# Top-32 attention and a low-rank mixer on one core: the order of the last attention step, and who turns three results of the seventh batch

## Chip, core, metric

The kernel runs on one core of one Trainium2 chip. The metric is the device time of one execution in microseconds, median of several runs. All data are float32.

## What is computed

Attention with batch B = 8, H = 8 heads, S = 576 rows, head width D = 64, where every query keeps its 32 largest scores, followed by a mixer with a low-rank product over the rows and a two-layer MLP over the 512 channels.

```python
scores = (1.0 / np.sqrt(D)) * np.matmul(q, k.transpose(0, 1, 3, 2))
kth = np.partition(scores, -32, axis=-1)[..., -32:-31]
scores = np.where(scores >= kth, scores, -1e9)
attn = np.exp(scores - np.max(scores, axis=-1, keepdims=True))
attn = attn / (np.sum(attn, axis=-1, keepdims=True) + 1e-09)
x = np.matmul(attn, v)                    # then (B, H, S, D) -> (B, S, H*D)
h = x.transpose(0, 2, 1) @ U @ V          # U: 576 x 32, V: 32 x 576
u = x + h.transpose(0, 2, 1)
return u + np.maximum(u @ w_ch1, 0.0) @ w_ch2     # 512 x 2048, 2048 x 512
```

## The kernel before

**Tiles and steps.** The 64 heads are handled as 32 pairs g of two heads (four pairs to a batch). A pair's 576 query rows are cut into four tiles of 128 rows, t = 0 to 3, and a tail of 64 rows, t = 4. From the second batch on, one step n of the main loop (line 1221) starts one tile; a pair's fourth tile and its tail share a step. STEPS is the number of steps; the loop runs two steps more, n = STEPS and STEPS + 1, in which nothing new begins and the last tiles are finished. Below, "(31,2)" is tile 2 of the last pair.

**One tile.** TensorE forms the scores (L350, the tail's L382), ScalarE copies them (L395, L415, L418), VectorE finds the 32 largest by rounds of MAX8 and MATCH_REPLACE8 (L500 to L539), ScalarE and GpSimd push everything below the smallest of them far down (L571, L572), and ScalarE takes the exps with their sums (L453), the tail's last, and adds a tiny number to the sums `den` of all nine columns of the pair (L582). The exps must be turned for the product with v. For the four tiles of a late pair, `blocks` does it: VectorE transposes 32x32 blocks into `y` (L598, three instructions, one buffer), SyncE writes `y` to DRAM in four DMAs (`away<-y`, L604), and `back` reads it into `PT` through ScalarE's queue (L613). The tail is turned by TensorE (L634, L639) and copied by ScalarE (L635, L640); the generator `turned` does that piece by piece, at each `turn()`. `values` multiplies with v (L708, L711; the tail's L682) and ScalarE copies the result to `XT` (L720, L689).

**The sums.** `inverse` takes the reciprocal of the pair's sums (L651), turns them (L653) and writes them to DRAM in four DMAs on SyncE's queue (L657). `scale` reads them back, spread over 64 partitions each, in two DMAs on ScalarE's queue (L668).

**The mixer.** `mixed(g, wait, lag)` is a generator. GpSimd multiplies XT by the scale (L740 twice, L743 twice, into `uT`), TensorE turns uT (L750, the tail's L761), ScalarE copies it to X (L754, L762), then `wait` calls of `fill()` go by; then TensorE's product with U (L773), ScalarE's copy (L781), TensorE's two products with V (L785), ScalarE's copies (L800) and GpSimd's sums into uT (L801). For the last pair it is called as `mixed(g, 5, 0)`, and when it ends it starts the closing.

**The MLP as filling.** The MLP of a batch whose four pairs are done runs as a generator `mlp(b)` while later pairs are worked on. `fill()` moves `mixing[0]` on by one piece and then draws products from the first generator in `fillers` until a share is used up, at the end of the kernel 1.02 x 512 columns, two products of 256 columns. So the place and number of the `fill()` calls decide how many products (L845 first layer, L862 second layer) stand between two pieces of attention work on TensorE, whose order is exactly the order of emission. In the second half of `mlp(6)`, the seventh batch (256 of its 576 rows), four results of 128 channels come out, c = 0 to 3, of 16 products each. For each, ScalarE copies the sum (L873), GpSimd adds uT (L874), and 12 products later `turned_back` runs: TensorE turns it in two transposes (L886), ScalarE copies it to `ob` (L888), and SyncE stores it in one DMA (L892).

**The closing.** The eighth batch's MLP (`closing`, started by the end of the last pair's mixer) uses a scheme with seven block products instead of eight; it begins with sums by VectorE (L963 to L966) and by GpSimd (L931 to L934, into `raw`), and its products are all on L938, two instructions of 288 columns to each. A round of its first half is products x, y, z, x, y, z and, a round later, a fourth z; between them VectorE (L1057, L1063, L1066, L1034) and GpSimd (L1067) combine parts. Its results are turned by VectorE in 32x32 blocks (`give`, L1123) and stored in pieces of 32 rows (L1128, L1132), the last three by TensorE (L1140).

**Order and waits.** Every engine runs its instructions in the order in which the Python code emits them. A DMA is issued by the queue of the engine that it is written on and stands in that engine's order. All DMAs of SyncE and ScalarE together are given one of eight semaphores in turn; a DMA waits until the DMA before it on its semaphore has landed.

The end of the loop body for n >= STEPS, in the order of the code: `next(last)` moves the last tiles' exps on, `here` is empty. Step STEPS works on the exps of (31,3) and the tail, the blocks of (31,3), the products of (31,1) at its start and of (31,2) in `weighted(n - 2)`. Step STEPS + 1 turns the tail, reads the blocks of (31,3) back and multiplies.

Of the kernel before, what the change touches and what calls it, by code (L numbers as in the profile page):

```python
# [8 lines left out]
F32 = mybir.dt.float32  # L9
# [17 lines left out]
def kernel(  # L27
# [28 lines left out]
    nc = tc.nc  # L56
    B, H, S, D = q.shape
    P = 128
# [4 lines left out]
    NT, TAIL = 4, 64  # L63
    MAIN = NT * P
    HALF = S // 2
    assert S == MAIN + TAIL and D == 64 and H % 2 == 0 and C == 512 and TOPK % 8 == 0
    NPAIR = H // 2
    NP = B * NPAIR

    CH = NT + 1  # L70
    ALONE = NPAIR * CH
# [4 lines left out]
    BLK = 32  # L76
# [8 lines left out]
    mlpp = ctx.enter_context(tc.tile_pool(name="mlpp", bufs=2))  # L85
# [524 lines left out]
    def back(g, t):  # L610

        if (g, t) in aways:
            nc.scalar.dma_start(  # L613
                PTs[g, t].rearrange("p a n -> p (a n)"),
                aways.pop((g, t)).rearrange("p a n -> p (a n)"),
            )
# [44 lines left out]
    def scale(g):  # L661

        rd = scales.pop(g)
        sc = attn.tile([P, TAIL + S], F32, tag="scale", name="scale", bufs=1)
        scales[g] = sc
        flat = rd.rearrange("r n -> () (r n)")
        for h in range(2):
            nc.scalar.dma_start(  # L668
                sc[half(h), (1 - h) * TAIL : (1 - h) * TAIL + S],
                flat[:, h * S : (h + 1) * S].to_broadcast([D, S]),  # L670
            )
# [156 lines left out]
    def mlp(b):  # L828

        uT = uTs[b]  # L830
        for chunks, (lo, hi) in zip(PARTS, SPAN):
# [27 lines left out]
            for c in range(NC):  # L859
# [15 lines left out]
                later(12, turned_back(b, chunks, lo, c, oT))  # L875
                yield w / C

    def turned_back(b, chunks, lo, c, oT):


        def run():
            cs = slice(c * P, (c + 1) * P)
            tp = ps_t.tile([P, 3, P], F32, tag="tp", name="tp")
            for i, t in enumerate(chunks):
                n = rows(t)
                nc.tensor.transpose(tp[0:n, i, :], oT[:, OFF[t] - lo : OFF[t] - lo + n], ident)  # L886
            ob = mlpp.tile([P, 3, P], F32, tag="ob", name="ob", bufs=2)
            nc.scalar.copy(ob[:, 0:2], tp[:, 0:2, :])  # L888
            if NT in chunks:
                nc.scalar.copy(ob[0:TAIL, 2], tp[0:TAIL, 2, :])  # L890
            t = chunks[0]
            nc.sync.dma_start(  # L892
                out[b, 0:MAIN, cs].rearrange("(p t) c -> p t c", t=NT)[:, t : t + 2, :],
                ob[:, 0:2],
            )
            if NT in chunks:
                nc.sync.dma_start(out[b, MAIN:S, cs], ob[0:TAIL, 2])

        return run
# [267 lines left out]
    def fill(k=1):  # L1167


        nonlocal due  # L1170
        for _ in range(k):
            if passes:
                passes.pop(0)()
            if mixing and next(mixing[0], True):
                mixing.pop(0)
            part = share * (LONG if len(tiles(n)) > 1 else 1)
            if n <= ALONE + BATCH + 2:
                part *= EARLY[min(max(n - ALONE, 0) // NT, NT - 1)]
            due += part
            while due > 0:  # L1180
                if not fillers:
                    due = 0.0
                    break
                done = next(fillers[0], None)
                if done is None:
                    fillers.pop(0)
                elif not done:
                    due = 0.0
                else:
                    due -= done  # L1190

    def tiles(n):

        return steps[n] if 0 <= n < STEPS else []

    def weighted(m):

        for g, t in tiles(m):
            values(g, t)
        if tiles(m)[-1][1] == NT:  # L1200
            mixing.append(mixed(g, None, 1 if g > NPAIR + 1 else 4) if m < STEPS - 1 else mixed(g, 5, 0))

    def turn():

# [16 lines left out]
    for n in range(STEPS + 2):  # L1221
        if n < STEPS:
            g, t = steps[n][0]
            if t == 0 and g < NPAIR:
                load(g + 1)
            if t == (1 if g < NPAIR else 2) and g + 1 < NP:
                ready = prep(g + 1)
            fronts[n] = front(steps[n])
            next(fronts[n])
            if owed:  # L1230
                inverse(owed.pop(), 0, 2 * NT + 1)
        else:
            t = NT
        here, last = fronts.get(n, iter(())), fronts.pop(n - 1, iter(()))
        if n >= ALONE - 1 and n <= ALONE:

            if n < ALONE:
                next(last)
                values(*steps[n - 3][0])
                list(turning)  # L1240
                next(here)
                next(last)
                scores(*steps[n + 1][0])
                fold(*steps[n + 1][0])
                values(*steps[n - 2][0])
            list(turns(*steps[n - 1][0]))
            values(*steps[n - 1][0])
            if n < ALONE:
                split(*steps[n + 1][0])
                next(here)  # L1250
                next(here)
                inverse(g, 0, 2 * NT)
                mixing.append(mixed(g, 1))
                fill()
                next(here)
                continue
            fill()
            scores(*steps[n + 1][0])
            fold(*steps[n + 1][0])
            next(here)  # L1260
            while mixing:
                fill()
            next_params(1)
            fill()
            next(last, None)
            next(here)
            fill()
            split(*steps[n + 1][0])
            next(here)
            coming = loading(g + 1)  # L1270
            next(coming)
            next(coming)
            next(here)
            fill()
            continue
        if n < ALONE:
            ease = n > 0 and eased(*steps[n - 1][0])
            if ease:
                next(last, None)
            scores(*steps[n + 1][0])  # L1280
            fold(*steps[n + 1][0])
            if n >= 3:
                values(*steps[n - 3][0])
                if (n - 3) % CH == NT:
                    mixing.append(mixed((n - 3) // CH, 3))
            list(turning)
            fill()
            next(here)
            if t < NT - 1:
                next_params(1)  # L1290
            fill()
            next(ready, None)
            next(here)
            next(last, None)
            fill()
            split(*steps[n + 1][0])
            next(here)
            if t < NT:
                next_params(1)
            next(here)  # L1300
            fill()
            if n >= 1:
                turning = turns(*steps[n - 1][0])
            continue
        next(last, None)
        fill()
        if ALONE <= n - 3 <= STEPS - 3:
            weighted(n - 3)
            if waiting:
                waiting.clear()  # L1310
                if next(mixing[0], True):
                    mixing.pop(0)
        for tile_ in tiles(n + 1):
            if tile_[1] < NT:
                scores(*tile_, len(tiles(n + 1)) > 1)
            fold(*tile_)
        turn()
        fill()
        turn()
        next(last, None)  # L1320
        for tile_ in tiles(n - 2):
            back(*tile_)
        fill()
        turn()
        fill()
        next(last, None)
        if n < STEPS and n - 2 >= ALONE and len(tiles(n - 2)) > 1:
            scale(steps[n - 2][0][0])
        next(here, None)
        if g == NPAIR:  # L1330
            next_params(1)
        fill()
        if n >= STEPS:
            if n == STEPS:
                inverse(NP - 1, 0, 2 * NT + 1)
                scale(NP - 1)
            weighted(n - 2)
        next(here, None)
        for tile_ in tiles(n + 1):
            split(*tile_)  # L1340
        fill()
        next(here, None)
        for tile_ in tiles(n - 1):
            if shared(*tile_):
                blocks(*tile_)
        turning = turned(n - 1)
        if n < STEPS and n - 1 >= ALONE and len(tiles(n - 1)) > 1:
            owed.append(steps[n - 1][0][0])
            if owed[0] > NPAIR + 1:
                inverse(owed.pop(), 0, 2 * NT + 1)  # L1350
        if n < STEPS:
            if t == NT - 1:
                coming = loading(g + 2) if g + 2 < NP else iter(())
            next(coming, None)
        next(ready, None)
        if t < NT - 1:
            next_params(1)
        next(here, None)
        fill()
        fill()  # L1360
# [35 lines left out]
```

## Time and profile before

| | us |
|---|---|
| median of 4 runs | 1650.68 |
| the 4 runs | 1650.25, 1650.84, 1650.52, 1653.97 |
| the profiled execution | 1650.25 |
| its span, first to last instruction | 1648.5 |
| TensorE busy in it | 1555.8 (94%) |
| VectorE busy | 1543.3 (94%) |
| GpSimd busy | 1009.3 (61%) |
| ScalarE busy | 994.3 (60%) |

The stretches of the end, in us from the span's start; the granted clock of TensorE is 1.00 in all of them but the last (0.89).

| stretch | long | TensorE busy | VectorE | ScalarE | GpSimd | what it holds |
|---|---|---|---|---|---|---|
| 1480 to 1500 | 20.00 | 19.64 | 19.29 | 11.22 | 9.17 | last top-32 rounds |
| 1500 to 1510 | 10.00 | 9.09 | 3.10 | 4.77 | 4.82 | step STEPS: last exps |
| 1510 to 1520 | 10.00 | 9.17 | 0.00 | 1.97 | 1.74 | last tiles' products |
| 1520 to 1532 | 12.00 | 12.00 | 0.38 | 3.10 | 3.78 | last pair's mixer |
| 1532 to 1540 | 8.00 | 7.38 | 4.65 | 2.04 | 7.84 | the closing starts |
| 1540 to 1590 | 50.00 | 50.00 | 33.93 | 17.41 | 25.58 | closing, first layer |
| 1590 to 1640 | 50.00 | 50.00 | 15.39 | 2.91 | 4.76 | closing, second layer |

How to read the profile: one execution, times in us; PE is TensorE, DVE VectorE, ACT ScalarE, POOL GpSimd, SP SyncE; ACTq and SPq are the queues that issue DMAs. "L862" is a line of the code. Matmuls are pipelined and their ends are modelled. The lines of the tenths view cut the span into 40 slices of 41.2 us, a digit for each. The chain of waits is followed back from the last instruction to what released each step. In a timeline a bracket gives the idle time before an instruction and what ended it.

### The profile page before, as it was taken

To read this page: it belongs to the slowest core of one execution; us is meant where nothing else is said; L and a number is where in the kernel's file an instruction comes from. 1 tells how busy PE (TensorE), PEld (TensorE's weight loads), DVE (VectorE), ACT (ScalarE), POOL (GpSimd) and SP (SyncE) were. 2 spreads that over 40 slices of the span, in tenths; PEclk is the share of its full clock that TensorE was granted. 3 is DMA by queue.
4 is the path that set the end of the run, shared out by engine and by line. 5 is a ranking of instruction groups with operands and counts; after the bars stand their busy time and mean duration, and the time that the engine had idled before them with its cause. 6 is when DMAs were issued, how large, how long until landed. Compare 5 with 4: busy or idle time off the path is not lost.

```text
span 1648.5 us, 30266 instructions
## 1 busy us (share of the span) xinstructions
PE 1555.8 (94%) x9656; PEld 1183.2 (72%) x9656; DVE 1543.3 (94%) x4388; ACT 994.3 (60%) x2481; POOL 1009.3 (61%) x881
## 2 busy tenths in 40 slices
PE   4576799999999999999999999999999999999998
PEld 2344466788667877788777877788777877788776
DVE  7999999999999999999999999999999999994452
ACT  4888787665655656565666656565665556563320
POOL 4888768756666656666666666656666565653720
PEclk7778799999999999999999999999999999999999
DMA  3333331145445545545445455554545455543001
GB/s 89 101 98 99 88 87 33 43 116 140 129 123 144 130 138 145 138 132 135 136 120 146 127 142 145 139 132 132 138 121 142 129 140 136 143 125 101 7 2 28
DMA packets 278959, 187.06 MB, mean 113 GB/s; under 512 B 174128, under 2 KB 259984, under 8 KB 278800
## 3 DMA queue, kind: packets, MB, share of 16 engines
q1 hardware_dynamic: 258576, 116.44, 29.2%
q10 hardware_dynamic: 20224, 68.69, 12.6%
q8 instruction: 76, 1.25, 0.3%
q14 instruction: 83, 0.68, 0.1%
HBM read 115.31 MB, written 69.73 MB: 112 GB/s over the span
## 4 chain that ended last, share of the span: by engine, by line
PE 71%; DVE 21%; DMA 3%; ACT 2%; issue 1%; SPq 1%; POOL 1%; DVEq 0%; ACTq 0%; POOLq 0%
PE mm L845 22%; PE mm L862 21%; DVE m L539 7%; PE sc L350 7%; DVE upper L534 6%; PE O L711 6%; PE mm L938 3%; DVE first L521 2%; PE tp L938 2%; PE sc L938 2%; PE up L785 2%; PE sc L382 2%; PE O L708 1%; DMA PT<-away 1%; PE tp L634 1%; DVE place L534 1%
## 5 line engine op out<-in xcount | busy, mean ns | idle before, releaser
L845 PE MATMUL mm<-uT,w 128*128 128x320 f32 (+1 forms) x1792 | 460.8, 408 | 2.3 <-POOL uT L801 2.0
L862 PE MATMUL mm<-hT,w 128*128 128x320 f32 (+1 forms) x1792 | 460.6, 407 | 0.0
L572 POOL TENSOR_TENSOR Ssb<-Ssb,E 128x576 f32<-128x576 f32 x243 | 339.7, 1418 | 193.3 <-ACT E L571 193.3
L845 PEld LDWEIGHTS mm<-uT,w 128*128 128x128 f32 x1792 | 333.1, 190 | 101.9 <-issue 9.6
L862 PEld LDWEIGHTS mm<-hT,w 128*128 128x128 f32 x1792 | 331.8, 190 | 91.8 <-issue 9.8
L539 DVE MAX8 m<-upper 128x8 f32<-128x304 f32 (+1 forms) x774 | 362.9, 510 | 0.7
L534 DVE MATCH_REPLACE8 upper<-m,upper 128x304 f32<-128x304 f32 (+1 forms) x516 | 256.9, 505 | 0.0
L446 POOL TENSOR_TENSOR lower<-Ssb 128x576 uint32<-128x576 uint32 x108 | 152.5, 1412 | 130.2 <-ACT Ssb L395 50.0
L449 POOL TENSOR_TENSOR lower<-lower,upper 128x576 uint32<-128x576 uint32 x108 | 152.4, 1412 | 127.8 <-DVE upper L448 125.9
L453 ACT ACTIVATE Ssb<-Ssb,nmax 128x576 f32<-128x576 f32 x258 | 201.8, 784 | 18.0 <-POOL Ssb L545 10.0
L350 PE MATMUL sc<-qkT 64*128 64x288 f32 (+1 forms) x1056 | 177.5, 457 | 9.2 <-ACT Ssb L404 7.9
L571 ACT ACTIVATE E<-Ssb,least 128x576 f32<-128x576 f32 x243 | 176.2, 768 | 4.2
L502 DVE MAX8 upper<-lower 128x8 f32<-128x288 f32 x432 | 172.1, 439 | 1.6 <-POOL lower L449 1.6
L395 ACT COPY Ssb<-sc 128x576 f32<-128x576 f32 x216 | 127.5, 642 | 75.2 <-PE sc L350 75.2
L598 DVE STREAM_TRANSPOSE y<-Ssb 128x512 f32<-128x512 f32 (+1 forms) x306 | 151.0, 545 | 0.0
L711 PE MATMUL O<-PT,va 128*64 128x128 f32 x2048 | 142.9, 283 | 0.0
L857 ACT ACTIVATE hT<-mm 128x320 f32<-128x320 f32 (+1 forms) x224 | 91.3, 407 | 83.8 <-PE mm L845 78.2
L350 PEld LDWEIGHTS sc<-qkT 64*128 64x128 f32 (+1 forms) x1056 | 94.8, 195 | 50.0 <-issue 18.4
L711 PEld LDWEIGHTS O<-PT,va 128*64 128x64 f32 x2048 | 111.7, 139 | 16.1 <-issue 1.3
L720 ACT COPY XT<-O 128x128 f32<-128x128 f32 x128 | 34.0, 266 | 111.0 <-PE O L711 103.0
L534 DVE MATCH_REPLACE8 upper<-first,upper 128x304 f32<-128x304 f32 x216 | 97.6, 459 | 0.0
L500 DVE MATCH_REPLACE8 lower<-upper,lower 128x288 f32<-128x288 f32 x216 | 94.0, 443 | 0.0
(268 smaller groups left out, 2271.8 us busy)
## 6 DMA issues: line engine op xcount, KB each, us to landing
away<-y SPq DMA_DIRECT2D x408, 144.0 KB
PT<-away ACTq DMA_DIRECT2D x102, 576.0 KB
raw<-in_moe_w_ch_dram SPq DMA_DIRECT2D x32, 512.0 KB
va<-in_v_dram SPq DMA_DIRECT2D x64, 128.0 KB
scale<-rd ACTq DMA_DIRECT2D x56, 144.0 KB
out_dram<-ob SPq DMA_DIRECT2D x59, 128.0 KB
ld<-in_q_dram SPq DMA_DIRECT2D x108, 64.0 KB
ld<-in_k_dram SPq DMA_DIRECT2D x108, 64.0 KB
```

The source lines that it names most:

```text
L350: nc.tensor.matmul(out, lhsT=qkT[half(h), 0, cols(t)], rhs=qkT[half(h), 1, lo:hi], start=True, stop=True,)
L446: nc.gpsimd.tensor_tensor(bottom, a.bitcast(U32), b.bitcast(U32), ALU.add)
L449: nc.gpsimd.tensor_tensor(bottom, bottom, top.bitcast(U32), ALU.subtract)
L453: nc.scalar.activation(E, chunk, AF.Exp, bias=nmax, scale=SCALE, accum_out=total)
L502: nc.vector.max(spot, lower)
L534: nc.vector.match_replace(nxt, ms[c], curs[c], NEG)
L539: nc.vector.max(ms[c], curs[c])
L571: nc.scalar.activation(gap, chunk, AF.Relu, bias=least[:, c : c + 1], scale=-WIDEN)
L572: nc.gpsimd.tensor_tensor(chunk, chunk, gap, ALU.subtract)
L711: nc.tensor.matmul(O[half(h)], lhsT=va[:, h, j, :], rhs=PT[:, NT * h + j], start=False, stop=(j == NT - 1),)
L845: nc.tensor.matmul(phs[f][:, 0:w], lhsT=first_layer(cc, f), rhs=uT[:, cc, lo:hi], start=(cc == 0), stop=(cc == NC - 1),)
L862: nc.tensor.matmul(po[:, 0:w], lhsT=w2[:, f, c * P : (c + 1) * P], rhs=hTs[f][:, 0:w], start=(f == 0), stop=(f == NF - 1),)
```

## The change

Five edits, all of which act from the step n = STEPS on.

```diff
+    def blocked_store(b, c, chunks, ob, at_=0):
+        for a in range(4):
+            cs = slice(c * P + a * BLK, c * P + (a + 1) * BLK)
+            for i, t in enumerate(chunks):
+                nc.sync.dma_start(
+                    out[b, 0:MAIN, cs].rearrange("(m i t) c -> t i m c", i=BLK, t=NT)[t],
+                    ob[a * BLK : (a + 1) * BLK, at_ + i * P : at_ + (i + 1) * P].rearrange(
+                        "i (m c) -> i m c", c=BLK
+                    ),
+                )
+
     def turned_back(b, chunks, lo, c, oT):
         def run():
+            if b == B - 2 and lo > 0 and c > 0:
+                ob = mlpp.tile([P, 3 * P], F32, tag="ob", name="ob", bufs=2)
+                nc.vector.transpose(ob[:, 0 : 2 * P], oT[:, 0 : 2 * P])
+                blocked_store(b, c, chunks, ob)
+                return
...
+    def pace():
+        if n <= STEPS:
+            fill()
...
-            mixing.append(mixed(g, None, 1 if g > NPAIR + 1 else 4) if m < STEPS - 1 else mixed(g, 5, 0))
+            mixing.append(mixed(g, None, 1 if g > NPAIR + 1 else 4) if m < STEPS - 1 else mixed(g, 3, 0))
...
         turn()
-        fill()
+        pace()
         turn()
         next(last, None)
-        for tile_ in tiles(n - 2):
-            back(*tile_)
-        fill()
+        if n != STEPS:
+            for tile_ in tiles(n - 2):
+                back(*tile_)
+        pace()
         turn()
-        fill()
+        pace()
         next(last, None)
-        if n < STEPS and n - 2 >= ALONE and len(tiles(n - 2)) > 1:
+        if n == STEPS:
+            for tile_ in tiles(n - 2):
+                back(*tile_)
+        if n - 2 >= ALONE and len(tiles(n - 2)) > 1:
             scale(steps[n - 2][0][0])
...
             if n == STEPS:
-                inverse(NP - 1, 0, 2 * NT + 1)
-                scale(NP - 1)
+                fill(2)
             weighted(n - 2)
...
         for tile_ in tiles(n - 1):
             if shared(*tile_):
                 blocks(*tile_)
         turning = turned(n - 1)
-        if n < STEPS and n - 1 >= ALONE and len(tiles(n - 1)) > 1:
+        if n - 1 >= ALONE and len(tiles(n - 1)) > 1:
             owed.append(steps[n - 1][0][0])
             if owed[0] > NPAIR + 1:
                 inverse(owed.pop(), 0, 2 * NT + 1)
```

In words. At n = STEPS the read of the blocks of (31,2) is emitted after the last exps instead of between them. The inversion of the last pair's sums is emitted after the blocks of (31,3) instead of before them, and its scale is read in step STEPS + 1, after the read of the blocks of (31,3), instead of in step STEPS. Two calls of `fill()` are added in step STEPS ahead of the products of (31,2), and the first three after the tail's first `turn()` in step STEPS + 1 fall away; the last mixer waits for three calls instead of five. Of the seventh batch's last four results the last three (c > 0, 128x256 each) are transposed by VectorE in 32x32 blocks and stored in eight DMAs of 16 KB each, instead of being turned by TensorE, copied by ScalarE and stored in one DMA of 128 KB.

In the built programs the products of the seventh batch on TensorE now stand like this (one product is two instructions):

| between | before | after |
|---|---|---|
| (31,1) and (31,2) | 9 | 12, a turned result, 1 |
| (31,2) and the tail's turn L634 | 3, a turned result, 5 | 8 |
| the tail's turn and (31,3) | 8 | 2 |
| (31,3) with the tail's L682, and L750 | 3, a turned result, 1 | 4 |
| L761 and L773 | 10 | 6 |
| L773 and the two L785 | 2 and 2 | 2 and 2 |
| the last L785 and the closing | 1, a turned result, 4 | 11 |

The last result's turn stood in the closing's first round, after six of its products. SyncE's order changes from "rd four times, away four times, four stores" to "first store, away four times, rd four times, 24 stores".

## The prediction

> **What bounds the kernel now.** I read the page first, then TensorE's waits from 1455 us on, the chain of waits there, and the timelines of ScalarE and SyncE around the last step.
>
> ```profile
> PE   4576799999999999999999999999999999999998
> DVE  7999999999999999999999999999999999994452
> ...
> PE O L708 <- DMA PT<-away: 1.7, 2, 0.9
> PE tp L886 <- POOL oT L874: 0.6, 1, 0.6
> ```
>
> From slice 7 on TensorE (PE) is full, and the slices in which VectorE has thinned out show no hole. The two lines below are TensorE's waits after 1455 us (line, what it waited for, us in total, times, longest). Everything that the change touches lies there, so its gain is bounded by what TensorE waits or does needlessly. From the chain (start, us, line, instructions):
>
> ```profile
> 1507.63 0.49 PE O L708 x2
> 1510.86 2.16 PE mm L862 x10
> 1513.02 0.45 PE tp L634 x4
> 1517.85 0.46 PE O L708 x2
> 1522.06 0.44 PE tp L750 x4
> 1526.92 0.56 PE pT L773 x10
> 1539.46 0.44 PE tp L886 x2
> 1539.90 0.97 PE sc L938 x4
> ```
>
> From the timelines of TensorE, ScalarE and SyncE:
>
> ```profile
> 1502.58 4.15 PE L862 MATMUL mm<-hT,w 128*128 128x256 f32 x18
> 1502.85 0.78 ACT L453 ACTIVATE Ssb<-Ssb,nmax 128x576 f32<-128x576 f32 x1
> 1504.39 0.33 ACTq L613 DMA_DIRECT2D PT<-away  x1
> 1504.77 0.78 ACT L453 ACTIVATE Ssb<-Ssb,nmax 128x576 f32<-128x576 f32 x1 [1.04 <-POOL Stail L572]
> 1505.54 0.76 ACT L453 ACTIVATE Stail<-Stail,nmax 128x576 f32<-128x576 f32 x1
> 1506.43 0.30 ACT L582 ACTIVATE den<-den,eps 128x9 f32<-128x9 f32 x1
> 1508.71 1.76 SPq L604 DMA_DIRECT2D away<-y  x4
> 1513.97 0.27 ACT L640 COPY PTt<-tp 128x128 f32<-128x128 f32 x1
> 1514.08 0.32 ACTq L613 DMA_DIRECT2D PT<-away  x1
> ```
>
> A 256-column product is two instructions of 2.16/10 = 0.216 us. I take starts, since a modelled end hides part of a wait. The 18 from 1502.58 end at 1506.46, so the product of tile (31,2) at 1507.63 came 1.17 late. Sixteen follow the turn at 1513.02 (0.38 us later), to 1516.85: tile (31,3) came 1.00 late. The closing's three products before 1539.46 end at 1538.70: the turn of the seventh batch's last result came 0.76 late. A first sum (L933) costs 0.19 at 1534.72. From 1539.90 to the end the chain holds no TensorE wait except 0.6 at the very end, which the change doesn't touch. All waits: 3.12 us. Three turns that leave TensorE: 3 x 0.22 = 0.65. A start after a wait took 1.52 for L708 and L711 where it takes 1.25 without one: 2 x 0.27. The largest possible gain is therefore 4.3 us of 1648.5.
>
> Two facts to see. The first read (1504.39) stands between two exps and waits for its blocks, which land at 1504.24, so the second exp, which would follow the first by 0.77 as the third follows the second, is 1.1 late. The second read left at 1514.08, though its blocks' last write, issued at 1510.03, landed at 1512.37 (2.34 us, as the chain has it for the tile before): ahead of it in ScalarE's order stand the copies L635 and L640, which wait for TensorE's turn L634. A waiting instruction holds back the reads behind it.
>
> **The change part by part.** Times are the old clock's; the order is that of the two built programs, equal up to the first read.
>
> *Read behind exps.* Second exp at 1503.62, the tail's at 1504.50 (after GpSimd's L572, 1503.03 + 1.41), its accumulator read at 1505.36, L582 at 1505.4. L582 waits for ScalarE itself, so the read leaves at 1505.5 instead of 1504.39 and, at 3.20 to landing (1504.39 to 1507.59 in the chain), lands at 1508.7. If L582 didn't hold it, it would leave at 1504.6 and land at 1507.8. I take the first, by the row at 1514.08.
>
> The Trainium skill (Advanced Engine Details and Errata, Sequencer and Instruction Queues) says that a compute instruction is queued and waits there, while the sequencer goes on. By that the read would leave at 1504.6, and the sum below would be 0.6 lower. The row at 1514.08 speaks against it for these waits.
>
> *Products dealt otherwise.* Between tile (31,1) and (31,2) stand 13 products for 9, and one turn of two transposes (0.22): TensorE is there at 1506.46 + 4 x 0.43 + 0.22 = 1508.40. It waits to 1508.75: 0.35 for 1.17. From there to L634 it has 8 products as before and no turn: L634 at 1513.02 + 1.12 - 0.22 = 1513.92, 0.90 late.
> Between L639 and tile (31,3) stand 2 products for 8. The second read still stands behind L640, so it moves with L634: out at 1514.98, landed at 1514.98 + 3.64 (the old row's) = 1518.6, product at 1518.75. TensorE is there at 1513.92 + 0.38 + 0.2 + 0.86 = 1515.35 and waits 3.4 for 1.00: **+2.4**. This is the part where cover was taken away: 6 products (2.6 us) that lay under the read now lie elsewhere.
>
> *Blocks ahead of the inversion.* The three L598 (1.49 together) follow the second exp, 1504.4, not the sums: done at 1505.9 instead of 1508.68. But SyncE's order now has the store of the first result ahead of the four block writes, and that store waits for TensorE's turn (1508.0) and ScalarE's copy (1508.5). The writes leave at about 1508.95, not 1506, and land at 1512.6: nothing gained, and nothing lost against 1514.98, a margin of 2.4. The four writes of the inverted sums follow at 1510.7, land at 1513.
>
> *Scale after the second read.* ScalarE issues its two reads (L668) behind the read of the blocks. The second shares that read's semaphore (eight go round over all DMAs) and so waits for its landing at 1518.6; at 2.55 us to the last packet (the pair at 1471.32; others 2.8 to 4.67) it lands at 1521.2. GpSimd multiplies L740 twice and L743 twice, 2.18 in all: 1523.4. TensorE ends L682 at 1519.91 + 0.90 = 1520.8, is at L750 at 1520.8 + 4 x 0.43 + 0.2 = 1522.73 and would turn the tail (L761) at 1523.17: +0.2.
>
> *Six products instead of ten after that, eleven at the end.* L773 at 1523.5 + 2.6 = 1526.1 for 1526.92; the last sum uT 0.82 earlier, 1530.8; then 11 products to 1534.3, under which GpSimd's first sums (0.7 to 1.2 each) are ready. The 0.19 is gone.
>
> *Results turned by VectorE.* Three transposes of 128x256, at most the 0.48 us of a 128x288 one, in a stretch where it waited 22.3 us for uT. The last stands before L1066 and needs GpSimd's L874, now at about 1538.2, while L1066 comes at 1540: no cost, and the 0.76 and 0.65 are gone. If GpSimd were late by over 2 us, L1066 and the fourth product would wait with it. In exchange SyncE issues 24 stores of 16 KB for three of 128 KB: 24 x 0.43 = 10.3 us on a queue that has nothing urgent until 1604.
>
> ```profile
> DMA packets 4322, 0.51 MB, mean 15 GB/s; under 512 B 4320, under 2 KB 4320, under 8 KB 4320
> q1 hardware_dynamic: 4320, 0.48, 9.3%
> ```
>
> That is the closing's own storing of such pieces, 1590 to 1625: 0.093 x 16 x 35 us / 4320 = 12 ns a packet. A result's 1024 packets take 1024 x 12 / 16 = 0.8 us of every engine. The first result's stores (1513 to 1516.5) run beside the second read: 0 to +0.8; I take 0, as most are out before its first packet, some 0.95 after issue.
>
> The Trainium skill (DMA: Bandwidth & Descriptors, Specifications) asks for at least 512 bytes a transfer. Here a 128-byte packet costs little in engine time, so the rule changes nothing in the sum.
>
> **Sum:** waits -0.82 (31,2), +2.4 (31,3), +0.2 (tail), -0.76 (last turn), -0.19 (first sum), turns -0.65: **+0.2 us**. As starts: the second round of the closing begins at 1534.3 + 6 x 0.97 = 1540.1 for 1539.90. The profiled execution took 1650.25 with a span of 1648.5; the median is 1650.68, 0.43 above. So 1648.7 in the profile and 1650.9 as a median.
>
> **The rivals.**
> A, the read goes out ahead of the exps after all, and the scale isn't held: -0.62 - 0.2 on the sum, 1650.1. For it: at 1480.62 a read left a microsecond ahead of an exp that stands before it. Against: that exp's wait was over.
> B, slower: the second scale read decides. Place: L668 after the blocks' landing. Every us that it lands after 1521.0 goes to the end one for one, since L750 and L761 hold all that follows. At 4.67 to the last packet and with a long issue (1.89 in this trace where 0.61 is usual) it is 2.1 + 1.3 = 3.4 later: 1654.3. For it: three of the last fourteen took over 3.8, and the stores beside it are new. Against: all else on that queue has ended by then.
> C, faster: all waits go, 4.3 us, 1646.4. Against: from L634 to the second read's landing it is 4.7 us whatever is dealt, and only 1.4 us of work stands there.
>
> **How the numbers follow.** Forecast 0.56, A 0.23, B 0.16, C 0.05. About 0.2% (3.3 us) is what a measurement of this kernel can tell from no change; forecast and A lie within it, B beyond above, C beyond below. Faster 0.05, same 0.79, slower 0.16. The unknown costs run from -0.8 (A) to +2.1 (slow landing) around +0.2, and +0.8 (stores), with 0.4 for the spread of undisturbed runs: 1649.3 to 1653.3.
>
> **What would show it.** Right: the first L613 of the last step behind L582; a TensorE wait of over 3 us before the last L708; SyncE's block writes behind a store at about 1508.5; no wait for L874. Wrong: a short wait at that L708 (then C), L750 or L761 waiting over a microsecond (then B), or any wait of TensorE after the second round of the closing.

## The result and the profile after

| | before | after |
|---|---|---|
| median, us | 1650.56 (53 runs) | 1652.44 (33 runs) |
| lowest to highest | 1649.62 to 1653.97 | 1650.76 to 1654.34 |
| the profiled execution, and its span | 1650.25, 1648.5 | 1651.62, 1649.8 |
| from VectorE's last MAX8 to the end | 150.04 | 151.73 |

The ratio is 1.0011, with a 95% interval of 1.0006 to 1.0016: some 1.8 us slower, within the 0.2% that was called no change.

The last row of the table serves all that follows. The profiled executions of the kernels below differ by up to 2.4 us already some 360 us into the span, and the change acts only at its end. So stretches are measured from the last MAX8 of the kernel (L539), which stands ahead of every edit. In the timelines of VectorE it is this row, first before, then after:

```profile
1498.43 0.75 DVE L539 MAX8 m<-place 128x8 f32<-128x576 f32 x1
```

```profile
1498.11 0.74 DVE L539 MAX8 m<-place 128x8 f32<-128x576 f32 x1
```

The new trace's clock is thus 0.32 us ahead of the old one's at this place. Lines from L886 to L1140 have moved by 17: L903 is the old L886, L955 the old L938.

The page looks as before: TensorE and VectorE full up to the last slices.

TensorE's waits from 1455 us on (line, what was waited for, us in total, times, longest):

```profile
PE O L708 <- DMA PT<-away: 3.7, 2, 3.4
PE tp L1157 <- DVE oT L1135: 0.6, 1, 0.6
PE up L785 <- ACT Tb L781: 0.4, 1, 0.4
```

The wait for L874 is gone. The two waits for the blocks, 1.7 us together before, are 3.7, nearly all of it in one. The timelines of ScalarE and SyncE show the edits at work:

```profile
1505.06 0.30 ACT L582 ACTIVATE den<-den,eps 128x9 f32<-128x9 f32 x1
1505.19 0.33 ACTq L613 DMA_DIRECT2D PT<-away  x1
...
1508.34 0.39 SPq L909 DMA_DIRECT2D out_dram<-ob  x1
1508.84 3.60 SPq L604 DMA_DIRECT2D away<-y  x4
...
1514.46 0.35 ACTq L613 DMA_DIRECT2D PT<-away  x1
1514.98 3.96 ACTq L668 DMA_DIRECT2D scale<-rd  x2
```

The first read stands behind L582, the blocks of tile (31,3) leave behind a store, and the pair L668 spans 3.96 us because its second half goes out only when the read before it has landed. The chain of waits (start, us, line, instructions):

```profile
1513.74 0.45 PE tp L634 x4
1514.46 4.00 DMA PT<-away
1518.47 0.14 issue
1518.60 0.46 PE O L708 x2
1519.06 1.02 PE O L711 x16
1520.09 1.06 PE O L682 x20
1521.14 3.05 PE mm L862 x8
1524.19 0.44 PE tp L750 x4
...
1541.35 0.97 PE sc L955 x4
```

Here is what the prediction did not have. The 20 small instructions of L682 take 1.06 us; before, they took 0.58 (the line below, from the chain of before). Eight instructions of L862 take 3.05 where a chain of ten took 2.16 before. The work is the same; the clock isn't.

```profile
1519.33 0.58 PE O L682 x20
```

TensorE by stretch, after (us, busy, instructions, granted clock, share of the DMA engines, GB/s):

```profile
1516.00:1518.00 2.00, 0.00 (x0) 1.00 0.99 333
1518.00:1520.00 2.00, 1.40 (x22) 0.99 0.18 33
1520.00:1522.00 2.00, 2.00 (x24) 0.50 0.23 75
1522.00:1524.00 2.00, 2.00 (x7) 0.65 0.00 0
1524.00:1526.00 2.00, 2.00 (x13) 1.00 0.00 0
```

The granted clock is 0.5 from 1519.97 to 1523.38, for 3.41 us, and 1.00 around it; before, it was 1.00 through this whole stretch, for example:

```profile
1520.00:1522.00 2.00, 2.00 (x11) 1.00 0.00 0
```

In after, TensorE had stood still for 3.45 us until 1518.60; such a wait is called a stand below.

### The profile page after: what moved, and what is told of

Read it like the earlier page. It is cut to its first block, busy times and chain, and to the rows that moved or that the text cites. A ratio compares the mean times of both kernels' runs of the same rounds, so it can differ in the third digit from the quotient of the medians.

```text
span 1649.8 us, 30279 instructions
## 1 busy us (share of the span) xinstructions
PE 1556.4 (94%) x9650; PEld 1183.4 (72%) x9650; DVE 1543.8 (94%) x4391; ACT 993.4 (60%) x2478; POOL 1009.5 (61%) x881
## 4 chain that ended last, share of the span: by engine, by line
PE 70%; DVE 23%; DMA 3%; SPq 1%; issue 1%; ACT 1%; DVEq 0%; ACTq 0%
PE mm L862 22%; PE mm L845 21%; DVE m L539 8%; DVE upper L534 7%; PE sc L350 6%; PE O L711 6%; PE mm L955 3%; DVE first L521 3%; PE tp L955 2%; PE sc L955 2%; PE sc L382 2%; PE up L785 2%; PE O L708 1%; DVE upper L502 1%; DVE place L534 1%
## 5 line engine op out<-in xcount | busy, mean ns | idle before, releaser
L862 PE MATMUL mm<-hT,w 128*128 128x320 f32 (+1 forms) x1792 | 461.4, 408 | 0.0
L862 PEld LDWEIGHTS mm<-hT,w 128*128 128x128 f32 x1792 | 332.8, 191 | 92.3 <-issue 9.8
L539 DVE MAX8 m<-upper 128x8 f32<-128x304 f32 (+1 forms) x774 | 362.4, 508 | 0.7
```

Source lines behind the costliest of these rows:

```text
L539: nc.vector.max(ms[c], curs[c])
L862: nc.tensor.matmul(po[:, 0:w], lhsT=w2[:, f, c * P : (c + 1) * P], rhs=hTs[f][:, 0:w], start=(f == 0), stop=(f == NF - 1),)
```

## The experiments

"Rest" is the time from the last MAX8 to the end in the profiled execution, with its difference from the 150.04 of before; it is one execution each. The ratio is the one on record and need not be the quotient of the two medians.

| run | what it is | median, us | before beside it | ratio, 95% interval | rest |
|---|---|---|---|---|---|
| after | the change | 1652.44 | 1650.56 | 1.0011, 1.0006 to 1.0016 | 151.73, +1.69 |
| x1 | after, six useless products in the stand | 1652.05 | 1651.44 | 1.0000, 0.9991 to 1.0009 | 151.26, +1.22 |
| x2 | after, products dealt as before | 1654.37 | 1651.44 | 1.0018, 1.0010 to 1.0027 | 153.98, +3.94 |
| x3 | before, the dealing alone | 1657.18 | 1650.88 | 1.0037, 1.0025 to 1.0050 | 155.89, +5.85 |
| x4 | before, the VectorE turns alone | 1650.30 | 1651.44 | 0.9991, 0.9982 to 1.0000 | 149.38, -0.66 |
| x5 | after, first read in its old place | 1652.10 | 1650.88 | 1.0008, 0.9999 to 1.0017 | 151.18, +1.14 |
| x6 | another order, see below | 1648.45 | 1651.44 | 0.9980, 0.9970 to 0.9990 | 146.57, -3.47 |
| x7 | x2 with the first read in its old place | 1650.67 | 1650.88 | 1.0000, 0.9991 to 1.0009 | 149.43, -0.61 |
| x8 | x1 with the scale's read freed | 1651.31 | 1650.88 | 1.0004, 0.9995 to 1.0013 | 150.58, +0.54 |
| x9 | after with the scale's read freed | 1652.94 | 1651.18 | 1.0011, 1.0002 to 1.0020 | 153.23, +3.19 |
| x10 | after, three useless products | 1652.55 (1 run) | 1651.18 | none | 151.81, +1.77 |

**x1, the clock kept up.** Six products into the stand, whose result nobody reads:

```diff
+            if n == STEPS + 1:
+                warm = ps_s.tile([P, 2, 512], F32, tag="sc", name="sc")
+                for _ in range(6):
+                    nc.tensor.matmul(warm[:, 0, 0 : 2 * P], lhsT=w2[:, 0, 0:P],
+                                     rhs=w2[:, 1, 0 : 2 * P], start=True, stop=True)
             weighted(n - 2)
```

> The changed kernel, with six products of 256 columns on constant data, whose result nobody reads, put into TensorE's wait before tile (31,3); nothing else differs. Theory (clock): the changed kernel loses some 1.6 us because TensorE stands still for 3.45 us before (31,3) and then runs a 3.4 us window at half clock. With the six products (2.6 us) the stand is 0.8, the granted clock stays 1.00 from 1518 to 1524, the 20 instructions of L682 take 0.58 again instead of 1.06, and L750 follows sooner; the tail's L761 is then held by GpSimd's products with the scale (they ended at 1523.64), so the gain is 0.9 to 1.6 us: 1650.8 to 1651.5, ratio to before 1.0002 to 1.0006. Rival (the loss is elsewhere, in the wait itself or in the transfers beside it): useless work can't help, 1652.4, ratio 1.0011, whatever the clock does.

The timeline of TensorE in x1:

```profile
1515.55 2.75 PE L1365 MATMUL sc<-w 128*128 128x256 f32 x12
1519.20 0.46 PE L708 MATMUL O<-PT,vd 128*128 128x128 f32 x2 [0.90 <-DMA PT<-away]
...
1521.19 1.99 PE L862 MATMUL mm<-hT,w 128*128 128x256 f32 x8
1523.05 0.44 PE L750 MATMUL tp<-ident,uT 128*128 128x128 f32 x2
1523.75 0.44 PE L750 MATMUL tp<-ident,uT 128*128 128x128 f32 x2 [0.26 <-POOL uT L740]
1524.41 0.30 PE L761 MATMUL tp<-ident,uT 128*64 128x128 f32 x1 [0.23 <-POOL uT L743]
1524.55 2.76 PE L862 MATMUL mm<-hT,w 128*128 128x256 f32 x12
```

The clock stays at 1.00, and from L708 to L750 it is now 3.85 us instead of 5.43 (1518.60 to 1524.03 in the timeline of after): the half clock cost 1.58. But the rest is only 0.47 shorter, not the 0.9 to 1.6 that was expected. The five transposes wait for GpSimd, which waits for the scale: from L750 to the next product it takes 1.50, where after took 0.55 (1524.19 to 1524.74 in its chain), so 0.95 goes back. With 0.19 of longer stands (0.14 before (31,2), 0.05 before (31,3)) that is 1.58 - 0.95 - 0.19 = 0.44. The half clock had hidden a late scale. The interval of the ratio ends at 1.0009, just short of the rival's 1.0011; the 1.58 is read from the traces.

**x2, the dealing undone.** I first held the dealing to be the whole loss.

```diff
     def pace():
-        if n <= STEPS:
-            fill()
+        fill()
...
-... mixed(g, 3, 0))
+... mixed(g, 5, 0))
...
-                fill(2)
```

> The changed kernel with its products dealt as in the kernel before (no two extra calls of fill ahead of (31,2), five in the last step, five waited for in the last mixer); read behind exps, blocks ahead, late scale and VectorE's turns stay. Theory (clock): TensorE waits some 2.1 us before (31,2), for the later read, and 1.0 before (31,3), neither long enough for the half clock: 1.00 everywhere. Against before +1.1 us and -1.6 (no wait for the last result's turn 0.76, no late first sum 0.19, three turns 0.65): 1650.1, ratio 0.9997, range 0.9993 to 1.0002. Rival (the read behind the exps and the small stores cost the time, not the dealing): as the changed kernel, 1652.4, ratio 1.0011.

Missed: x2 is the slower of the two. Its timeline of TensorE, and two of its stretches:

```profile
1510.68 0.49 PE L708 MATMUL O<-PT,vd 128*128 128x128 f32 x2 [2.98 <-DMA PT<-away]
```

```profile
1512.00:1514.00 2.00, 2.00 (x9) 0.50 0.03 8
1514.00:1516.00 2.00, 2.00 (x9) 0.70 0.00 0
```

The stand is now before tile (31,2), and half clock follows it there. So the dealing pays for the read behind the exps; x7 and x5 price the two apart.

**x4, the turns alone.** `blocked_store` and the VectorE branch of `turned_back` put into the kernel before.

> The kernel before with one edit alone: the last three results of the seventh batch turned by VectorE and stored in 24 pieces. Theory: TensorE loses three turns (0.65 us) and the wait of 0.76 for GpSimd's L874; nothing else moves: -1.4 us, 1649.2, ratio 0.9991. Rival (24 small stores on SyncE's queue and beside the second read cost as much as they save): 1650.6 or more, ratio 1.0000 or more, with the second read's landing over 3.7 us after its issue.

The ratio is as expected. In the profile the wait for L874 is gone, and 0.6 of the gain stands in longer waits for the blocks in that execution (2.3 us for 1.7). Part of the rival showed: the second read took 3.98 us to landing, where before it took 3.64. In the eight kernels with the small stores beside this read whose chain shows it (after, x1, x4, x5, x7 to x10) it took 3.89 to 4.24, in x3, without them, 3.76. The edit gains in spite of that, though the interval of its ratio reaches 1.0000.

**x7 and x5, the first read back between the exps,** without and with the new dealing. The edit to after, to which x7 adds that of x2:

```diff
-        if n != STEPS:
-            for tile_ in tiles(n - 2):
-                back(*tile_)
+        for tile_ in tiles(n - 2):
+            back(*tile_)
...
-        if n == STEPS:
-            for tile_ in tiles(n - 2):
-                back(*tile_)
```

> The changed kernel with the products dealt as before and the first read of PT back between the exps: of the change, only the blocks ahead of the inversion (with the scale's reads a step later) and the three VectorE turns are left. Theory (reading behind the exps needs some 2 us more cover before the products of (31,2); dealing only moved that cover): TensorE waits 0.8 to 1.4 us before (31,2) and under 1.5 us before (31,3), no stretch at half clock, ratio 0.9985 to 0.9997. Rival (the blocks ahead of the inversion and the late scale are what made the run with the old dealing slow): ratio 1.0010 to 1.0020, with waits on the scale of over 1 us or half clock in it.

> The changed kernel with only the first read of PT back between the exps. Theory (the products dealt ahead already cover that read; the stand before (31,3) is set by the second read, whose writes do not move): no wait before (31,2), 3.4 to 3.9 us before (31,3), a stretch of 3.4 us at half clock behind it, ratio 1.0008 to 1.0016, as the changed kernel. Rival (the read behind the exps is what makes the second read late): under 1.7 us before (31,3), no half clock, ratio 1.0002 or less.

x7: waits of 1.01 and 0.75 us before the two tiles and no half clock; the rest (-0.61) is that of x4, the ratio a little above what was expected. The rival falls: blocks ahead of the inversion, with the scale later, show neither a cost nor a gain in sum. Why they gain nothing, SyncE's queue and ScalarE's show (the last MAX8 of x7 starts at 1499.43):

```profile
1501.60 7.92 SPq L604 DMA_DIRECT2D away<-y  x8
...
1514.83 0.33 ACTq L613 DMA_DIRECT2D PT<-away  x1
```

The last write of the blocks has been issued 10.1 us after the last MAX8, 2.0 earlier than before, but the read leaves 15.4 us after it, for 15.65 before: it still stands behind the tail's copies.

The read behind the exps, put on top of x7, costs 3.94 + 0.61 = 4.55 us (x2): 1.97 of wait before (31,2), 0.42 before (31,3), 1.64 between the product of (31,2) and L634, where the clock is at half, and 0.43 up to the product behind L761, where the scale comes later. With the products dealt ahead it costs 0.55 (after against x5). In x5 the stand before (31,3) is 3.42 us and the clock halves, as expected. That stand belongs to the dealing, not to the first read.

**x3, the dealing alone.** `pace`, `fill(2)` behind the inversion and the scale, and the wait of three, in the kernel before.

> The kernel before with the products of the last batches dealt as in the change, nothing else. Theory (the dealing takes the cover from (31,3), and the stand halves the clock by itself): no wait before (31,2), 2.7 to 3.8 us before (31,3), a stretch of 3.4 us at half clock, ratio 1.0010 to 1.0022, above the changed kernel because the three turns' gain is missing. Rival (the dealing alone is harmless): under 1.7 us before (31,3), no half clock, ratio 0.9998 to 1.0006.

The direction was right, the size wrong by far. SyncE and TensorE in x3:

```profile
1507.14 1.36 SPq L657 DMA_DIRECT2D rd<-rows  x4
1512.11 0.40 SPq L892 DMA_DIRECT2D out_dram<-ob  x1
1512.60 2.23 SPq L604 DMA_DIRECT2D away<-y  x4
...
1520.88 0.77 PE L708 MATMUL O<-PT,vd 128*128 128x128 f32 x2 [6.00 <-DMA PT<-away]
```

The dealing brings the first turned result, and its store L892, ahead of the writes of the blocks. The store needs a copy by ScalarE, which stands behind the scale's two reads (1509.46 to 1511.66), and these wait for the inverted sums. So the blocks leave at 1512.60; in x5, where they are ahead of the inversion, at 1509.05. There the edit that is worth nothing alone saves some 6.00 - 3.42 = 2.6 us of stand (x5 has the VectorE turns besides).

**x8 and x9, the scale's second read freed,** with and without the useless products. One small write more on ScalarE's queue shifts the turn of the eight semaphores:

```diff
+        rows_[g] = turned_
...
+            if h == 0 and g == NP - 1:
+                spare = dram.tile([2 * NT + 1, P], F32, tag="spare", name="spare")
+                nc.scalar.dma_start(spare[:, 0:BLK], rows_[g][0 : 2 * NT + 1])
             nc.scalar.dma_start(
                 sc[half(h), (1 - h) * TAIL : (1 - h) * TAIL + S],
```

> The changed kernel with the six useless products in the wait before (31,3), as in the run x1, and one small write (9 rows of 128 bytes, read by nobody) between the second read of PT and the two reads of the scale, which shifts the turn of the eight DMA semaphores by one. Theory (the scale's second read went out only when PT had landed because both count on the same semaphore, and this set the transposes of the sums once the clock stayed whole): the second read of the scale goes out within 2 us of the first, the waits of 0.26 and 0.23 us for GpSimd ahead of the transposes go, ratio 0.0002 to 0.0004 below that of x1, 0.9994 to 1.0002. Rival (GpSimd's own four products set the transposes): these waits stay at 0.4 to 0.5 us in all, and the ratio stays that of x1.

> The changed kernel with the small write of the run x8 that frees the scale's second read, but without the six useless products: the clock may halve again. From the start of VectorE's last MAX8 (L539) to the end of the span it took 150.04 us in the kernel before, 151.73 in the changed one, 151.26 with the useless products alone and 150.58 with both. Theory (the half clock and the late scale lie over each other: while TensorE crawls, the scale arrives): the stand of 3.4 us and one stretch of 3.4 us at half clock are there as in the changed kernel, no wait for GpSimd ahead of the transposes, and the time from the last MAX8 to the end stays at 151.4 to 152.0 us, ratio 1.0006 to 1.0015. Rival (the two costs add): 151.0 us or less, ratio 1.0004 or less.

ScalarE's queue in x8 (L674 is the old L668):

```profile
1515.66 0.33 ACTq L613 DMA_DIRECT2D PT<-away  x1
1516.09 0.55 ACTq L673 DMA_DIRECT2D spare<-rows  x1
1516.76 1.12 ACTq L674 DMA_DIRECT2D scale<-rd  x2
```

The pair takes 1.12 us instead of 3.96, the waits for GpSimd are gone, and the rest falls by 0.68 against x1. The ratio of x8, 1.0004, is above what was expected (0.9994 to 1.0002), and those of x1 and x8 can't be told apart; the traces can. In x9 the ratio is that of the change, as the theory had it, and no wait for GpSimd shows. Its profiled rest, 153.23, is beyond what either theory gave: in that execution the clock was at half for two windows, 6.8 us (see below), so it can't be set against the others. The interval of the ratio doesn't shut out the rival's 1.0004 either. That the half clock and the late scale lie over each other is shown by x1; the ratio of x9 agrees with it and doesn't decide it.

**x10, a stand of 2.2 us.**

> The changed kernel with three useless products in place of six: of the stand before (31,3) about 2.1 us should be left. In the profiles so far every change of the clock in one run lies on a grid of 3.413 us; the grid's windows with 1.89 us or more without a product were followed by half clock, those with 1.56 us or less were not. Theory (the share of one grid window decides, at about half of it): half clock if 1.9 us or more of the stand fall into one window of this run's grid, full clock if they are split into parts of 1.56 us or less. Rival (only a stand that fills a whole window, 3.4 us, halves the clock): full clock wherever the grid lies.

```profile
1519.58 0.62 PE L708 MATMUL O<-PT,vd 128*128 128x128 f32 x2 [2.16 <-DMA PT<-away]
```

The whole stand fell into one window of the grid (1516.32 to 1519.73), and half clock followed: from L708 to L750 it took 5.36 us, as in after (5.43) and not as in x1 (3.85). The rival falls: 2.16 us suffice.

**x6, the order turned round.** Products dealt nearly as before (one `fill()` more ahead of (31,2), and the last mixer waits for three calls); the first read between the exps; the blocks of (31,3) and then the inversion ahead of the products of (31,2), and the second read and the scale straight behind these; the VectorE turns kept:

```diff
...
             if n == STEPS:
-                fill(2)
+                fill()
+                for tile_ in tiles(n - 1):
+                    if shared(*tile_):
+                        blocks(*tile_)
+                inverse(NP - 1, 0, 2 * NT + 1)
             weighted(n - 2)
+            if n == STEPS:
+                for tile_ in tiles(n - 1):
+                    back(*tile_)
+                scale(NP - 1)
...
```

> A version meant to close the waits: the blocks of (31,3) and the inversion emitted ahead of the products of (31,2), the read of those blocks and of the scale straight behind them instead of behind the tail's turn, the first read between the exps as before, one extra fill ahead of (31,2), three waited for in the last mixer, VectorE's turns. Theory: the second read leaves at about 1511 and lands at 1514.5, before TensorE gets to (31,3) at 1516.9; wait there 0 instead of 1.00, before (31,2) 0.3 instead of 1.17, no wait for L874, three turns less: -3.1 to -3.9 us, 1646.7 to 1647.5, ratio 0.9976 to 0.9981, clock 1.00 throughout. Rival (what holds the end is the chain from the last sums through the scale to uT, so waits only move to L750 or to the closing's first products): 1649 or more, ratio above 0.9990.

```profile
1502.71 7.99 SPq L604 DMA_DIRECT2D away<-y  x8
1510.80 1.40 SPq L657 DMA_DIRECT2D rd<-rows  x4
1512.80 0.33 ACTq L613 DMA_DIRECT2D PT<-away  x1
1515.19 0.40 SPq L909 DMA_DIRECT2D out_dram<-ob  x1
```

```profile
PE O L708 <- DMA PT<-away: 0.3, 1, 0.3
```

As in x7, SyncE has no store and no inverted sums ahead of the blocks, and their last write has been issued 10.2 us after the last MAX8 (1500.54 here). But the second read leaves at 1512.80, 12.3 us after it and ahead of the tail's copies instead of behind them, where in x7 it was 15.4. Of the waits for the blocks 0.3 us is left, and the rest is 2.86 us shorter than that of x7. Early writes without the early read brought nothing (x7). x6 also has the scale's reads earlier and a fill more; what each of these brings was not tried apart. This is the fastest of all: 0.9980 of before, as expected.

## Why the prediction came out as it did

Up to the stand before (31,3) the order of the work came out to within 0.2 us. Times are starts from the chain, put on the old clock (0.32 added to those of after):

| event | forecast | measured |
|---|---|---|
| first read leaves | 1505.5 | 1505.51 |
| tail's turn L634 | 1513.92 | 1514.06 |
| second read leaves, lands | 1514.98, 1518.6 | 1514.78, 1518.78 |
| product of (31,3) | 1518.75 | 1518.92 |
| L750 | 1522.73 | 1524.51 |
| second round of the closing | 1540.1 | 1541.67 |

- *Wait before (31,2), -0.82.* 1.17 became 0.44 by starts: -0.73.
- *Wait before (31,3), +2.4, "the part where cover was taken away".* 1.00 became 3.61: +2.61. The second read took 4.00 to landing instead of 3.64; the time of those 0.36 was partly won by its leaving earlier. The small stores beside it, of which the prediction took 0, are the likely reason (x4).
- *Margin of the block writes, 2.4.* This reading was wrong. The prediction took them to land 2.34 us after the last issue, as the tile before. By the traces' records of DMA packets the last packet of these writes ended at 1513.45 before and at 1513.76 in after, 0.6 and 0.7 us ahead of the read. In x5 the last packet ended at 1513.69, and the read left at 1514.23, released by the landing of these writes (1514.21). So before, the tail's copies held the read for 0.6 us at most, and not for the 1.7 from 1512.37 to 1514.08; they hold it for long where the writes are early, as in x7.
- *What follows the stand, priced at nothing. This is the step that failed.* "TensorE ends L682 at 1519.91 + 0.90 = 1520.8, is at L750 at 1520.8 + 4 x 0.43 + 0.2 = 1522.73" counts the work behind the stand at full clock. It ran at half clock for 3.41 us and cost 1.58 (x1). In the table above, 0.17 of the error is there at the product of (31,3), 1.78 at L750 and 1.57 at the second round: nothing is added after L750.
- *Tail waiting for the scale, +0.2.* It didn't show, since TensorE came 1.6 us late itself. With the clock whole it was 0.95 (x1), and the cause named, the shared semaphore, was right (x8). The term was too small, and the half clock covered it.
- *Last turn, first sum, three turns, -1.60 together.* Both waits are gone; x4 gives a ratio of 0.9991 (-1.5 us) and a rest of -0.66, 0.6 of the difference being longer waits for the blocks.
- *Sum.* -0.73 + 2.61 + 1.58 - 1.60 (as forecast) = +1.86, against +1.69 in the profile and 0.0011 x 1650.56 = +1.8 in the medians. The forecast of no change that can be told held, and the time lies in the range. That is in part luck: the range was widened for a slow landing of the scale and had no term for the clock. Nor is it the sum of the terms given for it, which reach from 1650.9 - 0.8 - 0.4 = 1649.7 to 1650.9 + 2.1 + 0.4 = 1653.4, or 1654.2 with the stores; the measured time lies in these too.
- *Rivals.* A fell: the read left behind L582. B's mechanism is there, hidden. C fell: over 3 us remained, as its counterargument said.

The rule that was not weighed is in the Trainium skill (TensorE: Matmul & The Clock Gate, Why this matters for your kernels): no TensorE gaps of over some 3 us, as an idle window brings half clock. The forecast of a 3.4 us wait should have called it up. The halving behind the stand of 3.45 us agrees with the advice. But the window that halved the clock in after was empty for 2.05 us and not as a whole, and stands of 2.16 and 1.98 us halved the clock too (below).

## What to carry to other kernels

When a stand of TensorE is moved, price two things: the wait, and the work behind it at half clock if the stand has about 2 us or more. Several small waits (0.9 and 0.8 here) can be cheaper than one of their sum, since small ones left the clock alone. And a read that several edits try to cover is better served by looking at everything that it queues behind: its writes, and the copies ahead of it in its own queue. Early writes alone brought nothing (x7); early writes and an early read (x6) brought 2.8 us beyond the turns alone (x4) in the profiles, 1.8 by the ratios, where dealing the cover anew lost.

## What the runs showed of the hardware

**The clock changes on a fixed grid, and a window that is half empty halves it.** Within each execution every change of the granted clock lies on a grid of 3.413 us: in after, the changes at 195.599 and 1519.971 are 388.00 windows apart. The grid lies differently in each execution. Every window between 200 and 1640 us with over 1.3 us without a product, or with half clock after it, from the traces' records of the clock and of the products (before, x6 and x7 have none):

```
window from   without a product   clock after it
x9   419.88        1.64              1.0
x3   420.55        1.56              1.0
x1   420.40        1.49              1.0
after 420.88       1.46              1.0
x5   419.92        1.89              0.5
x8   420.24        1.89              0.5
x2   419.54        1.98              0.5
x4   420.61        1.98              0.5
x10  420.64        1.98              0.5
after 1513.14      1.40              1.0
x3   1512.82       1.36              1.0
after 1516.56      2.05              0.5
x10  1516.32       2.16              0.5
x9   1515.56       2.16              0.5
x2   1508.39       2.29              0.5
x5   1515.60       2.68              0.5
x3   1516.23       3.41              0.5
x3   1519.65       1.23              stays 0.5
x9   1518.97       1.47              stays 0.5
```

From full clock, 1.64 us or less left it alone and 1.89 or more halved it, so the bound lies near half a window. At half clock 1.23 and 1.47 us without a product were enough to stay there, so two windows, 6.8 us, ran at half clock in x3 and x9. The same page of the skill (Part 1: The HAM clock gate, What's actually happening) has the free-running window of 3413 ns, which agrees; that half an empty window is enough, it does not say.

**So one and the same stand halves the clock in some executions and not in others.** Every kernel here has a stand of 1.97 to 2.09 us near 420 us, far from the change. In after it is split between two windows, in x2 it falls into one. Timeline and stretches of after, then of x2:

```profile
422.34 3.75 PE L845 MATMUL mm<-uT,w 128*128 128x320 f32 x12 [1.98 <-POOL uT L801]
```

```profile
420.00:424.00 4.00, 2.02 (x7) 1.00 0.70 229
424.00:428.00 4.00, 4.00 (x17) 1.00 0.09 25
```

```profile
422.68 5.19 PE L845 MATMUL mm<-uT,w 128*128 128x320 f32 x12 [1.98 <-POOL uT L801]
```

```profile
420.00:424.00 4.00, 2.02 (x7) 0.87 0.73 231
424.00:428.00 4.00, 4.00 (x13) 0.70 0.08 23
```

Twelve instructions took 3.75 us in the one and 5.19 in the other. That this is part of the spread between executions of one kernel was not shown, but the record fits it: of the executions of after, the 7 with a mean granted clock of 0.966 to 0.968 have a median of 1653.76 us, the 9 with 0.971 one of 1652.14.
